# Reordering the first 8 microseconds of a gated attention and MLP kernel: a transpose moved between two groups of products, and the first DMA transpose held longer

## The chip, the cores and the metric

The kernel runs on one core of a Trainium2 chip. The metric is the device time of one execution in microseconds (us). Two forms of it occur below. The *time* is what is compared between kernels. The *span* is what the hardware profiler covers in one profiled execution; the time of that same execution is about 1.7 us longer than its span.

Engines: PE multiplies matrices, PEld is its weight load, DVE and ACT are the vector and scalar engines, POOL is the general engine, SP does nothing here but issue DMAs (SPq in the profile). ACT issues a few DMAs too (ACTq).

## The reference, cut to what matters

```python
x: (1, 2048, 640) bf16
g = sigmoid((x * gate_w).sum(-1))                # gate
qkv = x @ wqkv; q, k, v = ...                    # 32 heads of 20
pk = phi(k)                                      # phi(t) = where(t > 0, t + 1, exp(t)) + 1e-6
kv = einsum("bhsd,bhse->bhde", pk, v)            # linear attention
...                                              # an MLP block b on layernorm(x)
return g * a + (1 - g) * b
```

The kernel starts with K = x @ wk, in 16 chunks of 128 rows of x. A product on PE needs x transposed (the contraction on the partitions), so each chunk has to be transposed, and it needs five slabs of 128 rows of wk.

## The kernel before: the parts that matter

Chunks 0 to 2 are loaded plainly and transposed on PE. Chunks 3 to 15 are transposed by DMA on their way in. All of `late_loads` is issued by SP, one after the other.

```python
for dc in range(3):
    load_wk(aq, dc)                 # K-weight slabs 0, 1, 2, issued by ACT (L162)
load_x(0, 1); load_x(1, 2); load_x(2, 3)        # x chunks 0, 1, 2, issued by SP (L152)
sp.dma_start(wkg[:, 3:5, 0:D], ...)             # slabs 3 and 4 (L169)

def k_mm(c, p, dc):                 # chunk c times slab dc: two matmuls, 512 and 130 columns (L255)
    ...

def late_loads():                   # DMA transposes are load_xT (L155)
    load_xT(3, 4); load_xT(4, 5); load_x(3, 4); load_xT(5, 6); load_xT(6, 7); load_x(4, 6)
    load_xT(7, 8); load_xT(8, 10); load_x(6, 9); load_xT(10, 11); load_xT(11, 13); load_x(9, 12)
    load_xT(13, 16); load_x(12, 16)
    sp.dma_start(wq, ...)           # Q weights (L296), then w1, wv, wo, w2
    ...

def x_tr(c, a, b):                  # chunk c's turn: 5 PE transposes (L321), then two copies
    for dc in range(DC):
        nc.tensor.transpose(t[:, ...], x_sb[:, c, ...], ident[:])
    nc.vector.tensor_copy(xT[:, 0:3, ...], ...)         # L322
    act(xT[:, 3:5, ...], ..., ACT.Copy)                 # L323

x_tr(0, 3, 2)
nc.vector.memset(xT[:, 0, 3 * P:3 * P + 1], 0.0)        # L328
late_loads()
x_tr(1, 1, 2)
k_mm(0, 0, 0); k_mm(1, 1, 0)
k_mm(0, 0, 1); k_mm(1, 1, 1)
x_tr(2, 3, 2)
k_mm(2, 2, 0); k_mm(2, 2, 1)
# ... slabs 2, 3, 4 of chunks 0 to 2; then chunks 3 to 15, with products L264 between; then Q (L388)
```

The memset is a brake. It writes one column of the place that the first DMA transpose (chunk 3) will fill, so that transpose has to wait until the memset is done, and with it everything behind it in SP's queue. The purpose is to keep the DMA transposes, which move in 256-byte packets, off the DMA engines while the first x chunks and slabs load.

## Time and profile before

| | before |
|---|---|
| time, median of 3 | 266.31 us (266.26 to 266.87) |
| time of the profiled execution | 267.08 us |
| span of the profiled execution | 265.4 us |
| PE busy | 259.8 us, 98% |

The busy line of the page of the kernel before (busy us, share of the span, instructions):

```profile
PE 259.8 (98%) x1666; PEld 134.8 (51%) x1666; DVE 127.2 (48%) x227; ACT 109.7 (41%) x163; POOL 35.5 (13%) x118
```

The timeline of PE in the first microseconds of the kernel before. Columns: start, duration, engine, source line, operation, output and inputs, shape, count; in brackets the idle time before it and what ended it.

```profile
4.03 0.62 PE L321 MATMUL pp<-ident,RXH 128*128 128x128 bf16 x5
4.91 0.49 PE L321 MATMUL pp<-ident,RXH 128*128 128x128 bf16 x5 [0.26 <-DMA RXH<-in_A_x_dram]
5.23 0.91 PE L255 MATMUL pp<-RA,RXT 128*128 128x512 bf16 x4
6.69 0.70 PE L255 MATMUL pp<-RA,RXT 128*128 128x512 bf16 x4 [0.55 <-DMA RA<-in_A_wqkv_dram]
7.23 0.44 PE L321 MATMUL pp<-ident,RXH 128*128 128x128 bf16 x5
8.15 0.65 PE L255 MATMUL pp<-RA,RXT 128*128 128x512 bf16 x3 [0.47 <-ACT RXT L323]
```

PE waits 0.55 us for slab 1, multiplies (6.69), transposes chunk 2 (7.23), and waits 0.47 us for the copies of that transpose. After 8.15 us it has no gap worth naming. (The idle time in brackets counts from the modelled end of the instruction before, so a wait costs a little more than it shows: chunk 2's last transpose starts at 7.46 us and the next product at 8.15, 0.69 us later, where transposes otherwise start 0.06 us apart.)

The DMA issues of the kernel before between 1.80 and 2.17 us (KB, then us from issue to landing): x chunk 2, issued at 1.72, and slab 1, issued at 1.79.

```profile
RXH<-in_A_x_dram SPq DMA_DIRECT2D x1, 160.0 KB, 4.7
RA<-in_A_wqkv_dram ACTq DMA_DIRECT2D x1, 160.0 KB, 4.9
```

So chunk 2 landed at 6.44 us and slab 1 at 6.65.

### The profile page before, as it was taken

What the parts mean: (1) busy time and instruction counts of PE and PEld (TensorE: products, weight loads), DVE (VectorE), ACT (ScalarE), POOL (GpSimd) and SP (SyncE); (2) the same over time, 40 slices, a digit from 0 to 9 for tenths busy, and PEclk for the clock granted to TensorE, in tenths of its full rate; (3) what the DMA queues carried; (4) which work ended last, traced back from release to release, by engine and by line L of the source; (5) the groups of instructions that cost most, each with busy time, mean ns of one, the idle gap of its engine ahead of it and who ended that gap; (6) DMA issues with size and microseconds to landing.
All of it is one profiled execution on the core that took longest, in us unless ns stands there. A gap on an engine that the chain in (4) does not pass through costs nothing.

```text
span 265.4 us, 4180 instructions
## 1 busy us (share of the span) xinstructions
PE 259.8 (98%) x1666; PEld 134.8 (51%) x1666; DVE 127.2 (48%) x227; ACT 109.7 (41%) x163; POOL 35.5 (13%) x118
## 2 busy tenths in 40 slices
PE   6999999999999999999999999999999999999995
PEld 2555555555564445554444455555544444555552
DVE  2386659888995257999920044233200002233242
ACT  3466654555454771334977512022034444022020
POOL 7000043030200000446870000000000000000000
PEclk9999999999999999999999999999999999999999
DMA  6899994452252069992542001001000000001001
GB/s 197 162 207 236 367 252 95 99 52 49 50 57 44 11 160 385 340 137 49 108 94 49 0 2 49 25 27 49 27 25 0 0 2 0 25 27 49 25 27 49
DMA packets 42207, 23.95 MB, mean 90 GB/s; under 512 B 31052, under 2 KB 41420, under 8 KB 42188
## 3 DMA queue, kind: packets, MB, share of 16 engines
q1 hardware_dynamic: 41602, 23.16, 36.4%
q10 hardware_dynamic: 586, 0.53, 0.6%
q8 instruction: 13, 0.21, 0.3%
q14 instruction: 6, 0.05, 0.1%
HBM read 12.86 MB, written 3.44 MB: 61 GB/s over the span
## 4 chain that ended last, share of the span: by engine, by line
PE 96%; DMA 2%; DVE 0%; ACTq 0%; ACT 0%; issue 0%
PE pp L637 20%; PE pp L570 20%; PE pp L421 8%; PE pp L596 8%; PE pp L555 8%; PE pp L264 8%; PE pp L255 8%; PE pp L388 8%; DMA RA<-in_A_wqkv_dram 2%; PE pp L579 2%; PE pp L622 1%; PE pp L631 1%; PE pp L586 1%; PE pp L455 1%; PE pp L441 1%; PE pp L468 0%
## 5 line engine op out<-in xcount | busy, mean ns | idle before, releaser
L637 PE MATMUL pp<-RB,RXH 128*128 128x512 bf16 (+1 forms) x390 | 54.4, 299 | 0.0
L570 PE MATMUL pp<-lnxT,RA 128*128 128x512 bf16 x240 | 52.1, 379 | 0.0
L637 PEld LDWEIGHTS <-RXH 128*128 128x128 bf16 x390 | 29.6, 98 | 24.2 <-issue 2.1
L570 PEld LDWEIGHTS <-RA 128*128 128x128 bf16 x240 | 23.4, 98 | 28.1
L599 ACT ACTIVATE RXH<-pp,g_all 128x640 f32<-128x640 f32 x16 | 12.7, 794 | 54.9 <-PE pp L596 54.9
L572 ACT ACTIVATE RXH<-pp 128x1024 bf16<-128x1024 f32 x24 | 24.3, 1020 | 26.7 <-PE pp L570 26.7
L247 ACT ACTIVATE eb<-pp 128x640 bf16<-128x640 f32 (+1 forms) x26 | 21.4, 828 | 25.0 <-PE pp L388 16.1
L264 PE MATMUL pp<-RPK,RXH 128*128 128x512 bf16 (+1 forms) x160 | 25.2, 299 | 0.0
L255 PE MATMUL pp<-RA,RXT 128*128 128x512 bf16 (+1 forms) x160 | 24.1, 299 | 1.0 <-DMA RA<-in_A_wqkv_dram 0.5
L601 DVE SCALAR_TENSOR_TENSOR RPK<-RPK,omg,RXH 128x640 f32<-128x640 f32 x8 | 7.1, 885 | 36.5 <-ACT RXH L599 36.5
L388 PE MATMUL pp<-RXT,RA 128*128 128x512 bf16 x100 | 23.2, 379 | 0.0
L596 PE MATMUL pp<-Mp,pqT 128*128 128x512 bf16 (+1 forms) x160 | 23.1, 299 | 0.0
L555 PE MATMUL pp<-w,RXH 128*128 128x512 bf16 (+1 forms) x160 | 21.9, 299 | 0.0
L601 DVE SCALAR_TENSOR_TENSOR RXT<-RXT,omg,RXH 128x640 f32<-128x640 f32 x8 | 7.1, 885 | 24.6 <-ACT RXH L599 24.6
L421 PE MATMUL pp<-lnxT,RB 128*128 128x512 bf16 x80 | 18.3, 380 | 0.0
L264 PEld LDWEIGHTS <-RXH 128*128 128x128 bf16 x160 | 12.7, 98 | 10.4
L255 PEld LDWEIGHTS <-RXT 128*128 128x128 bf16 x160 | 12.4, 98 | 10.8 <-DVE RXT L322 0.9
L596 PEld LDWEIGHTS <-pqT 128*128 128x128 bf16 x160 | 12.2, 98 | 10.0 <-issue 0.8
L555 PEld LDWEIGHTS <-RXH 128*128 128x128 bf16 x160 | 12.3, 98 | 9.6
L606 DVE SCALAR_TENSOR_TENSOR RXH<-pp,omg,RXT 128x640 bf16<-128x640 f32 x8 | 7.1, 884 | 19.8 <-PE pp L637 19.8
L606 DVE SCALAR_TENSOR_TENSOR RXH<-pp,omg,RPK 128x640 bf16<-128x640 f32 (+2 forms) x9 | 7.3, 810 | 19.1 <-PE pp L637 17.2
L388 PEld LDWEIGHTS <-RA 128*128 128x128 bf16 x100 | 11.1, 117 | 9.1
(107 smaller groups left out, 251.4 us busy)
## 6 DMA issues: line engine op xcount, KB each, us to landing
out_dram<-RXH SPq DMA_DIRECT2D x15, 160.0 KB, 1.8
RA<-in_B_w_dram SPq DMA_DIRECT2D x5, 432.0 KB, 6.7
RA<-in_A_wqkv_dram SPq DMA_DIRECT2D x2, 800.0 KB, 6.8
RB<-in_B_w_dram SPq DMA_DIRECT2D x1, 1120.0 KB
RXH<-in_A_x_dram SPq DMA_DIRECT2D x2, 480.0 KB, 5.1
RB<-in_B_w_dram SPq DMA_DIRECT2D x1, 960.0 KB, 12.2
RB<-in_B_w_dram SPq DMA_DIRECT2D x1, 800.0 KB, 8.5
Mp<-Mscr SPq DMA_DIRECT2D x1, 800.0 KB
```

The costliest lines, as they stand in the source:

```text
L247: act(e[:, 0:n], src, ACT.Exp)
L255: mm(PP[p][:, n0:n1], lhsT=xT[:, dc, c * P:(c + 1) * P], rhs=wkg[:, dc, n0:n1], start=(dc == 0), stop=(dc == DC - 1))
L264: mm(PP[p][:, n0:n1], lhsT=x_sb[:, c, i * P:(i + 1) * P], rhs=pk[:, c, n0:n1], start=(c == 0), stop=(c == NCH - 1))
L388: mm(PP[p][:, tt * 512:(tt + 1) * 512], lhsT=wqp[:, dc, j], rhs=xT[:, dc, t0:t0 + 512], start=(dc == 0), stop=(dc == DC - 1))
L421: mm(PP[p][:, tt * 512:(tt + 1) * 512], lhsT=lh, rhs=lnxT[:, dc, t0:t0 + 512], start=(dc == 0), stop=(dc == DC - 1))
L555: mm(PP[p][:, n0:n1], lhsT=hsT[:, fc, 2 + c * P:2 + (c + 1) * P], rhs=w2[:, fc, n0:n1], start=(fc == 0), stop=(fc == DC - 1))
L570: mm(PP[p][:, k * 512:(k + 1) * 512], lhsT=w3[:, dc, (fc + k) * P:(fc + k + 1) * P], rhs=lnxT[:, dc, t * 512:(t + 1) * 512], start=(dc == ...
L572: act(h2T[:, t % 2, fc:fc + 2, :], PP[p][:].rearrange("p (k s) -> p k s", k=2), ACT.Gelu_apprx_tanh)
L596: mm(PP[p][:, n0:n1], lhsT=pqT[:, j, c * P:(c + 1) * P], rhs=Mp[:, j, n0:n1], start=(j == 0), stop=(j == DC - 1))
L601: nc.vector.scalar_tensor_tensor(x1(c), x1(c), omg[:, c:c + 1], ga, op0=ALU.mult, op1=ALU.add)
L606: nc.vector.scalar_tensor_tensor(oc[:, n0:n1], PP[p][:, n0:n1], omg[:, c:c + 1], x1(c)[:, n0:n1], op0=ALU.mult, op1=ALU.add)
L637: mm(PP[p][:, n0:n1], lhsT=h2T[:, k, fc, cc], rhs=w4[:, fc, n0:n1], start=False, stop=(fc == NF - 1))
```

## The change

The intent: PE does chunk 2's transposes between the slab-0 and the slab-1 products, where it would otherwise wait for slab 1, and the copies run while PE does the slab-1 products. In addition the brake is moved behind chunk 1's turn, so that the DMA transposes start later.

```diff
     x_tr(0, 3, 2)
+    x_tr(1, 1, 2)
     nc.vector.memset(xT[:, 0, 3 * P:3 * P + 1], 0.0)
     late_loads()
-    x_tr(1, 1, 2)
     k_mm(0, 0, 0)
     k_mm(1, 1, 0)
+    x_tr(2, 3, 2)
     k_mm(0, 0, 1)
     k_mm(1, 1, 1)
-    x_tr(2, 3, 2)
     k_mm(2, 2, 0)
     k_mm(2, 2, 1)
```

No instruction is added or removed.

## The prediction

> **What bounds the kernel now.** PE: busy 259.8 us of 265.4 (98%, page), 96% of the chain that ended last. The timeline shows no PE gap over 0.03 us between 8.15 us and the last matmul's end at 262.3 us. All that can be saved lies in the first 8.15 us, where the timeline has three gaps: 0.26 us before chunk 1's transposes (x chunk 1), 0.55 us from 6.15 to 6.69 ("DMA RA<-in_A_wqkv_dram": the second K-weight slab, landing at 6.65), and 0.47 us from 7.68 to 8.15 ("ACT RXT": the copies of chunk 2's turn).
>
> **What the change does.** It adds and removes nothing; the order comparison shows PE's five chunk-2 transposes moved ahead of four K matmuls, and one 59 ns DVE memset moved behind a copy.
>
> 1. Chunk 2's transposes issue 54 to 57 ns apart, 0.28 us for five (the Trainium skill, "TensorE: Matmul & The Clock Gate", Back-to-back issue gap, gives N/2.4 + 2.5 = 56 ns for N = 128; the trace agrees). They now start in the 0.55 us gap, but not at its head: x chunk 2, issued at 1.72 us, lands 4.7 us later by the DMA issue view, at 6.44. PE resumes 0.04 us after a landing, so they run from 6.48 to 6.76.
> 2. Slab-1 products follow: 6.76 to 7.30, against 6.69 to 7.23 before.
> 3. Chunk 2's first product needs both copies. In the trace it starts 0.97 us after the first transpose's weight load (7.18 to 8.15). So 6.48 + 0.97 = 7.45 us instead of 8.15; PE idles 0.15 us instead of 0.47.
> 4. Then 0.54 us of products, and slab 2 is needed at 7.99; it landed at 7.95 before. That just fits. From 6.45 us on 256-byte transpose packets share the DMA engines with the last slab rows; holding them should make slab 2 land earlier.
>
> Gain: 0.70 us, all on the critical path, as PE is gapless afterwards.
>
> **What it costs.** The memset now follows the copy of chunk 1 (5.28 us) instead of chunk 0 (4.57), so the first DMA transpose issues 0.7 us later (4.97 to 5.7). SP issues these back to back (1.2 to 1.3 us per chunk), so the whole load chain slips by 0.7 us while PE comes 0.7 us earlier: each load loses 1.4 us of slack. Landing against first use now: chunk 3 8.55 and 11.1, chunk 5 11.6 and 13.8, chunk 7 15.4 and 17.8, chunks 13 to 15 25.5 and 27.6, Q weights 30.6 and 32.5. The thinnest slack is 1.9 us, so 0.5 us remains. I expect no new wait, but this is the main risk.
>
> **Predicted time:** 266.31 - 0.70 = 265.6 us, 265.1 to 266.3 in 8 of 10. Faster by over 2%: 0.5%; within 2%: 99%; slower by over 2%: 0.5%.
>
> **What would show each step.** Timeline: chunk 2's transposes start near 6.5 us; slab-1 products without a DMA wait; a wait of 0.1 to 0.2 us for the copies; PE gapless from 7.45 us; last matmul near 261.6 us; first DMA transpose issued near 5.7 us; PE idle after 4 us down from 1.3 to about 0.6 us.
>
> **What would make it wrong.** If x chunk 2 lands after 6.65, each tenth costs a tenth of the gain; if by 6.2, the gain could reach 0.9. If slab 2 lands later than 8 us, the wait moves there. If chunk 5, 7, 13 or the Q weights land late, a wait for "RXT<-in_A_x_dram" or "RA<-in_A_wqkv_dram" appears between 10 and 33 us and gives the gain back. The runs before spread 0.6 us, nearly the gain.

## The result

| | before | changed |
|---|---|---|
| time, median of 6 | 266.36 us (266.26 to 266.87) | 265.96 us (265.91 to 266.60) |
| ratio | | 0.9989, interval 0.9976 to 1.0003 |
| span of the profiled execution | 265.4 us | 264.2 us |

A ratio is the mean time of one kernel's fast runs over that of the other's of the same rounds, so it is not quite the ratio of the medians. All runs quoted here were fast, except one of the kernel before in the last group (270.57 us), which the ratios leave out.

The medians differ by 0.40 us, the spans of the two profiles by 1.2. This contradiction is the first thing to explain.

The busy line of the page of the changed kernel, and its PE timeline at the start (32 matmul records are missing from this trace, which is why PE's sum is lower):

```profile
PE 257.8 (98%) x1634; PEld 134.8 (51%) x1666; DVE 127.1 (48%) x227; ACT 109.7 (42%) x163; POOL 35.9 (14%) x118
```

```profile
5.06 0.27 PE L321 MATMUL pp<-ident,RXH 128*128 128x128 bf16 x2 [0.30 <-ACT RXT L323]
5.17 0.71 PE L255 MATMUL pp<-RA,RXT 128*128 128x512 bf16 x4
5.82 0.45 PE L321 MATMUL pp<-ident,RXH 128*128 128x128 bf16 x5
6.11 2.08 PE L255 MATMUL pp<-RA,RXT 128*128 128x512 bf16 x11
```

The chunk-2 transposes now run at 5.82 us, and the products follow without the 0.47 us wait. But they start 0.66 us earlier than the prediction allowed, because chunk 2 landed at 5.77 us instead of 6.44. And chunk 1 had landed at 4.35 us instead of 4.86. Nothing in the change had run by 4.35 us: its first effect is the moved memset, after 4.8 us. So part of the difference between the two profiles is not of the change.

### The profile page after: what moved, and what is told of

Read it like the earlier page. It is cut to its first block, busy times and chain, and to the rows that moved or that the text cites. A ratio compares the mean times of both kernels' runs of the same rounds, so it can differ in the third digit from the quotient of the medians.

```text
span 264.2 us, 4148 instructions
## 1 busy us (share of the span) xinstructions
PE 257.8 (98%) x1634; PEld 134.8 (51%) x1666; DVE 127.1 (48%) x227; ACT 109.7 (42%) x163; POOL 35.9 (14%) x118
## 4 chain that ended last, share of the span: by engine, by line
PE 95%; DMA 2%; issue 1%; ACTq 1%; DVE 0%
PE pp L637 20%; PE pp L570 20%; PE pp L421 8%; PE pp L596 8%; PE pp L264 8%; PE pp L555 8%; PE pp L388 8%; PE pp L255 8%; DMA RA<-in_A_wqkv_dram 2%; PE pp L579 2%; PE pp L622 1%; PE pp L631 1%; PE pp L586 1%; PE pp L455 1%; PE pp L441 1%
## 5 line engine op out<-in xcount | busy, mean ns | idle before, releaser
L637 PE MATMUL pp<-RB,RXH 128*128 128x128 bf16 (+1 forms) x382 | 53.9, 298 | 0.4
L255 PE MATMUL pp<-RA,RXT 128*128 128x130 bf16 (+1 forms) x156 | 23.8, 297 | 0.3
L555 PE MATMUL pp<-w,RXH 128*128 128x128 bf16 (+1 forms) x157 | 21.7, 297 | 0.2
```

What stands on the lines that cost most here:

```text
L255: mm(PP[p][:, n0:n1], lhsT=xT[:, dc, c * P:(c + 1) * P], rhs=wkg[:, dc, n0:n1], start=(dc == 0), stop=(dc == DC - 1))
L555: mm(PP[p][:, n0:n1], lhsT=hsT[:, fc, 2 + c * P:2 + (c + 1) * P], rhs=w2[:, fc, n0:n1], start=(fc == 0), stop=(fc == DC - 1))
L637: mm(PP[p][:, n0:n1], lhsT=h2T[:, k, fc, cc], rhs=w4[:, fc, n0:n1], start=False, stop=(fc == NF - 1))
```

## The experiments

The theory had two parts. **Theory C**: the profile of before caught an execution whose loads landed late. **Theory A**: the moved transposes carry the gain; **rival B**: the longer hold does. A third question came with the second group: what gives gain back later. **Theory D**: the load chain, started later, lands after PE is ready; **rival E**: the landing of the late loads is set by the DMA engines, not by when the chain starts.

Each group of four kernels ran on one chip, with runs of the kernel before among them; the groups ran on different chips. All twelve gave the right result.

For every profile I give the number that decides: the start of chunk 3's first weight load ("chunk 3"), the start of the Q products' first, and their difference. With no wait in between, PE needs 21.38 us for that stretch (eleven of the fourteen profiles show 21.38 or 21.39). What is over 21.38 is called *late wait* below. After the Q products start, every profile needs the same 229.8 to 229.9 us to the last matmul, so nothing later matters.

| profile | first DMA transpose issued | x chunk 2 landed | PE at full clock from | chunk 3 | late wait | Q weights landed | last matmul ends |
|---|---|---|---|---|---|---|---|
| before | 4.97 | 6.44 | 4.43 | 11.09 | 0 | 30.64 | 262.33 |
| changed | 5.20 | 5.77 | 4.29 | 9.93 | 0 | 30.66 | 261.17 |
| b_again | 4.98 | 5.27 | 5.05 | 10.27 | 0 | 30.33 | 261.51 |
| a_again | 5.51 | 5.27 | 5.30 | 9.74 | 0.76 | 31.83 | 261.72 |
| only_move | 4.97 | 5.65 | 4.79 | 9.73 | 0.32 | 31.38 | 261.27 |
| only_hold | 5.38 | 5.30 | 4.67 | 10.27 | 0 | 29.82 | 261.51 |
| m_again | 4.98 | 5.61 | 6.76 | 10.62 | 0 | 30.45 | 261.86 |
| m_nohold | 2.66 | 5.97 | 4.52 | 11.22 | 0 | 29.54 | 262.45 |
| m_early | 4.61 | 5.42 | 4.35 | 9.85 | 0 | 30.04 | 261.09 |
| a_hold2 | 7.42 | 5.74 | 6.87 | 10.51 | 2.08 | 32.07 | 263.82 |
| a_third | 5.51 | 7.42 | 6.44 | 11.33 | 0 | 30.76 | 262.57 |
| a_merge | 5.33 | 7.07 | 4.55 | 10.97 | 0 | 30.90 | 262.22 |
| me_again | 4.61 | 7.11 | 6.25 | 11.02 | 0 | 29.97 | 262.26 |
| me_merge | 4.61 | 5.34 | 5.39 | 9.96 | 0 | 29.79 | 261.20 |

(All in us from the start of the span. Landings are issue time plus the time to landing in the trace. The clock is the moment from which the trace records PE at its full clock.)

Two of these columns vary from execution to execution whatever the kernel: when chunk 2 lands, and when PE's clock goes to full speed. The earliest start of chunk 3 seen is then 10.27 us in the old order (b_again, only_hold) and 9.73 us in the new (only_move, a_again); a late landing or a late clock comes on top. Where chunk 2 landed late, after 6.4 us, the table shows a larger gain: chunk 3 starts 4.65 us after the landing in the old order (before) and 3.90 to 3.91 us after it in the new (a_third, a_merge, me_again), 0.74 us less.

### Group 1: both kernels again, and each half alone

**b_again.** No edit: the kernel before.

> The kernel before, unchanged, for a second profile and for the noise. The two profiles we have differ by 1.16 us in PE's last matmul, the times only by 0.4. Theory C (the first profile of before caught an execution in which the first loads landed late: x chunk 1 at 4.86 us against 4.35 in the changed kernel, before any moved instruction runs): the ratio to before is 1.000 within 0.0015, and a profile of a typical execution has x chunk 1 landing near 4.35, slab 1 near 6.0, and a last matmul near 261.5 us. Rival (the profile is typical and the change itself brought the landings forward): x chunk 1 lands near 4.86 again and the last matmul ends near 262.3.

Measured: 266.57 us against 266.64 for the kernel before in the same group, ratio 1.0003 (0.9990 to 1.0016). Chunk 1 landed at 3.95 us, chunk 2 at 5.27, slab 1 at 5.45, earlier still than expected. PE timeline of b_again:

```profile
5.22 0.27 PE L321 MATMUL pp<-ident,RXH 128*128 128x128 bf16 x2 [0.15 <-ACT RXT L323]
5.33 1.25 PE L255 MATMUL pp<-RA,RXT 128*128 128x512 bf16 x8
6.42 0.44 PE L321 MATMUL pp<-ident,RXH 128*128 128x128 bf16 x5
7.33 0.92 PE L255 MATMUL pp<-RA,RXT 128*128 128x512 bf16 x5 [0.47 <-ACT RXT L323]
```

The 0.55 us wait for slab 1 is gone in the same kernel; the eight products of slabs 0 and 1 run in one piece. Only the 0.47 us wait for the copies remains. Theory C holds: the first profile was of a late-landing execution, 0.82 us worse at the last matmul (262.33 against 261.51). Its time, 267.08 us against a median of 266.31, had said so from the start.

**a_again.** No edit: the changed kernel.

> The changed kernel, unchanged, for a second profile and a tighter time. If the prediction's sum (0.70 us) holds, the ratio to before is near 0.9974. If slab 2's landing now caps the gain, as its 0.09 us wait at 7.44 to 7.54 us in the first profile suggests, the gain is 0.3 to 0.5 us: 0.9981 to 0.9989. The profile should again show a short PE wait for slab 2 (the DMA of the K weights) before the slab-2 products, and none after.

Measured: 266.53 us against 266.64, ratio 0.9999 (0.9981 to 1.0016), with a wide spread (265.72 to 267.49). Both expected ratios were missed. By luck this profile has nearly the same landings up to slab 1 as b_again (chunk 1 at 3.90, chunk 2 at 5.27, slab 1 at 5.46), so the two can be laid side by side. PE timeline of a_again at the start:

```profile
5.21 0.29 PE L321 MATMUL pp<-ident,RXH 128*128 128x128 bf16 x2 [0.15 <-ACT RXT L323]
5.34 0.71 PE L255 MATMUL pp<-RA,RXT 128*128 128x512 bf16 x4
5.89 0.44 PE L321 MATMUL pp<-ident,RXH 128*128 128x128 bf16 x5
6.17 2.10 PE L255 MATMUL pp<-RA,RXT 128*128 128x512 bf16 x13
```

No gap of note after 5.21 us, and chunk 3 starts at 9.74 instead of 10.27: the front gain is 0.53 us. That is the length of the four slab-1 products (0.54 us), which now run while DVE and ACT copy. The short wait for slab 2 that I expected is absent (slab 2 landed at 6.68). But a_again ends 0.21 us *later* than b_again. The weight loads of a_again show why:

```profile
18.23 1.20 PEld L255 LDWEIGHTS <-RXT 128*128 128x128 bf16 x10 [0.29 <-DMA RXT<-in_A_x_dram]
26.81 1.20 PEld L255 LDWEIGHTS <-RXT 128*128 128x128 bf16 x10 [0.57 <-DMA RXT<-in_A_x_dram]
31.88 0.59 PEld L388 LDWEIGHTS <-RA 128*128 128x128 bf16 x4 [0.32 <-DMA RA<-in_A_wqkv_dram]
```

In b_again the same three have no wait:

```profile
18.58 1.24 PEld L255 LDWEIGHTS <-RXT 128*128 128x128 bf16 x10
26.75 1.24 PEld L255 LDWEIGHTS <-RXT 128*128 128x128 bf16 x10
31.65 0.82 PEld L388 LDWEIGHTS <-RA 128*128 128x128 bf16 x5
```

PE is 0.53 us ahead and then waits for the DMA transpose of chunk 8, for that of chunk 13 and for the Q weights. (A weight load's idle time includes a part that is there in any case, since loads run ahead of the products; the late wait proper is 0.76 us, from the table.) The gain was won at the front and given back at 18 to 32 us.

Only part of that lateness is of the longer hold. SP's chain starts 0.53 us after b_again's, but the Q weights landed 1.50 us later (31.83 against 30.33). The rest arises at one place: the DMA transposes of chunk 10 and of chunks 11 and 12, which SP issues one after the other. The SP timeline of b_again, then of a_again:

```profile
14.72 4.04 SPq L155 DMA_TRANSPOSE RXT<-in_A_x_dram  x2
```

```profile
15.22 5.22 SPq L155 DMA_TRANSPOSE RXT<-in_A_x_dram  x2
```

**only_move.** The transposes moved, the brake where it was before.

```diff
     x_tr(0, 3, 2)
-    x_tr(1, 1, 2)
     nc.vector.memset(xT[:, 0, 3 * P:3 * P + 1], 0.0)
     late_loads()
+    x_tr(1, 1, 2)
```

(This diff and the next ones are against the changed kernel, unless said otherwise.)

> Only the five PE transposes of chunk 2 moved; the first DMA transpose is released after chunk 0's copy, as before. Theory A (the moved transposes carry the gain): the ratio equals that of the changed kernel within 0.0005. Rival B (the hold carries it, because 256-byte transpose packets delay the last slab rows): slab 2 lands 0.3 us or more later than in the changed kernel, the wait before the slab-2 products grows by as much, and the gain is 0.1 us or less (0.9996 or more).

Measured: 266.03 us against 266.64, ratio 0.9979 (0.9967 to 0.9991). That is 0.0020 below the changed kernel's ratio, where theory A allowed 0.0005, so neither theory's ratio came true. Chunk 3 starts at 9.73, as early as in a_again, and the late wait is 0.32 us. Theory A holds for the front: the moved transposes alone bring it all. Rival B's mechanism is there in size (slab 2 landed at 7.30 against 6.68 in a_again, of which some may be the execution, as chunk 2 landed later too) but costs nothing to speak of, as PE gets to slab 2 only at about 7.3. SP's timeline of only_move has the same pair of DMA transposes:

```profile
14.68 5.41 SPq L155 DMA_TRANSPOSE RXT<-in_A_x_dram  x2
```

The chain started with b_again's (4.97 us against 4.98) and was level with it up to this pair, which took 1.37 us longer; the Q weights landed 1.05 us later. So the late wait of this profile does not come from a later start. In the other twelve profiles the pair took 3.7 to 4.2 us. Why it took over 5 us in these two is open.

**only_hold.** The brake moved, the transposes where they were; the diff is against the kernel before.

```diff
     x_tr(0, 3, 2)
+    x_tr(1, 1, 2)
     nc.vector.memset(xT[:, 0, 3 * P:3 * P + 1], 0.0)
     late_loads()
-    x_tr(1, 1, 2)
```

> Only the hold: the first DMA transpose waits for chunk 1's copy, PE order as before. Theory A: no gain, ratio 1.000 within 0.0005, since PE still transposes chunk 2 after the slab-1 products and waits about 0.47 us for the copies, and slab 2 has landed by then. Rival B: slab 1 or slab 2 lands earlier by 0.2 us or more and the gain is 0.2 us or more (0.9992 or less).

Measured: 266.66 us against 266.64, ratio 1.0004 (0.9987 to 1.0021). Chunk 3 starts at 10.27, exactly as in b_again, though slab 2 landed 0.34 us earlier (6.69 against 7.03). One pair could be chance, but the table's five profiles in which chunk 2 landed between 5.2 and 5.5 us bear it out: slab 2 landed at 7.41, 7.24, 7.03, 6.69 and 6.68 us where the first DMA transpose was issued at 4.61, 4.61, 4.98, 5.38 and 5.51. The hold does what it is meant to do to the DMA engines and wins nothing here. It agrees with the Trainium skill, "DMA: Bandwidth & Descriptors", Issuing engines are not separate DMA queues: DMAs run on the same 16 engines and interleave, whoever issued them. Slab 2 is issued by ACT, the transposes by SP, and where the transposes were held longer, slab 2 landed earlier.

### Group 2: the start of the load chain, from none to long

**m_again.** No edit to only_move.

> The move without the hold, again, on another chip, as the yardstick of this group. Theory D (the move gains about 0.53 us at the front; the later start of the load chain gives part of it back where chunk 8, chunk 13 and the Q weights land after PE is ready): ratio 0.9975 to 0.9988, PE gapless from about 5.2 us to chunk 13, waits of 0.1 to 0.4 us in all for chunk 13 and the Q weights.

Measured: 266.28 us against 266.76, ratio 0.9987 (0.9968 to 1.0006). In this profile x chunk 1 landed at 5.14 us, the latest of all, and PE reached its full clock only at 6.76. The view of the transposes' line, m_again from 5.0 to 5.75 us and then b_again from 5.1 to 6.5 (count, shortest, median and longest duration in ns), shows the same instruction at the two clocks:

```profile
L321 PE MATMUL pp<-ident,RXH x5: 287/314/314, 5.2 to 5.6; 128*128 128x128 bf16 x5
```

```profile
L321 PE MATMUL pp<-ident,RXH x4: 216/218/219, 5.2 to 6.5; 128*128 128x128 bf16 x4
```

The Trainium skill, "TensorE: Matmul & The Clock Gate", What's actually happening, says that PE starts at half clock and is released after about 3.4 us of activity, at a moment that depends on a free-running window. The trace agrees in kind: 314 ns and then 218, with the step 3.1 to 5.6 us after PE's first matmul at 1.24 us over the fourteen profiles.

So chunk 3 started only at 10.62, and there was no late wait at all. The expected waits did not come, and not only because PE was late. A PE that starts chunk 3 at 9.73 needs chunk 8 at about 18.04 us, chunk 13 at 26.21 and the Q weights at 31.11 (b_again's weight loads, less 0.54); here they landed at 18.00, 25.42 and 30.45. By the same sum only a_again, only_move and a_hold2, of the fourteen profiles, have landings that such a PE would have waited for. An early front makes a late wait longer, but there is none unless the load chain lands late.

**m_nohold.** The move, and no brake at all (diff against only_move).

```diff
     x_tr(0, 3, 2)
-    nc.vector.memset(xT[:, 0, 3 * P:3 * P + 1], 0.0)
     late_loads()
```

> The move, with the artificial memset taken away, so that SP issues the first DMA transpose near 2.7 us. Theory D: the waits for chunk 13 and the Q weights vanish (both land 1.5 to 2.3 us earlier), and what is lost instead is at the front: the 256-byte transpose packets share the DMA engines with x chunk 2 and slabs 1 to 4, which land 0.5 to 1.5 us later, so PE waits there. Net ratio 0.999 to 1.003. Rival E (late waits come from DMA saturation between 15 and 31 us and not from when the chain starts): Q weights land at the same time, 30.3 to 31.8 us, as in the others.

Measured: 266.32 us against 266.76, ratio 1.0001 (0.9972 to 1.0030), spread 265.72 to 268.37. PE timeline of m_nohold:

```profile
6.10 0.44 PE L321 MATMUL pp<-ident,RXH 128*128 128x128 bf16 x5
7.64 1.19 PE L255 MATMUL pp<-RA,RXT 128*128 128x512 bf16 x7 [1.10 <-DMA RA<-in_A_wqkv_dram]
```

Slab 1 landed at 7.60 us and PE waited 1.10 us for it. There is no late wait, as expected, but the front gain is gone too. That speaks for the brake; the times do not separate the two kernels (266.32 us against m_again's 266.28).

Its Q weights landed at 29.54 us, 0.9 before m_again's (30.45) and 1.8 before only_move's (31.38), though the chain started 2.3 us earlier. Neither theory holds strictly: they landed before those of all other profiles, but by less than the earlier start, and by how much differs from profile to profile.

**m_early.** The move, with the brake ahead of chunk 0's copy (diff against only_move).

```diff
+    nc.vector.memset(xT[:, 0, 3 * P:3 * P + 1], 0.0)
     x_tr(0, 3, 2)
-    nc.vector.memset(xT[:, 0, 3 * P:3 * P + 1], 0.0)
     late_loads()
```

> The move, with the memset ahead of chunk 0's copy instead of behind it: the first DMA transpose near 4.6 us, 0.37 earlier. Theory D: late waits shrink to 0.1 us or less, the front keeps its gain as the x and slab loads end near 6.4 to 7.3 us and the transposes' packets start near 6.1 us; ratio equal to the move alone or 0.0005 to 0.001 lower. Rival E: no change of the Q weights' landing.

Measured: 266.03 us against 266.76, ratio 0.9979 (0.9962 to 0.9996). The first DMA transpose is issued at 4.61 us, chunk 3 starts at 9.85, no late wait, and the last matmul ends at 261.09, the earliest of all profiles.

**a_hold2.** The changed kernel with a longer brake: the memset behind chunk 2's turn.

```diff
     x_tr(1, 1, 2)
-    nc.vector.memset(xT[:, 0, 3 * P:3 * P + 1], 0.0)
-    late_loads()
     k_mm(0, 0, 0)
     k_mm(1, 1, 0)
     x_tr(2, 3, 2)
+    nc.vector.memset(xT[:, 0, 3 * P:3 * P + 1], 0.0)
+    late_loads()
```

> The changed kernel with the hold made longer: the first DMA transpose waits for chunk 2's copy (about 6.6 us, 1.1 us later than in the changed kernel's second profile). Theory D: the added hold comes out nearly in full at the end, by longer waits for chunk 8, chunk 13 and the Q weights: last matmul 0.6 to 1.1 us after the changed kernel's, ratio 1.002 to 1.004. Rival E: the Q weights land as before and the ratio stays near 1.000.

Measured: 268.83 us against 266.76, ratio 1.0093 (1.0057 to 1.0129), clear of noise and over twice the loss that theory D expected. PE timeline of a_hold2:

```profile
14.45 1.54 PE L255 MATMUL pp<-RA,RXT 128*128 128x512 bf16 x10 [1.00 <-DMA RXT<-in_A_x_dram]
19.30 1.53 PE L255 MATMUL pp<-RA,RXT 128*128 128x512 bf16 x9 [0.87 <-DMA RXT<-in_A_x_dram]
```

PE waits for chunk 5 (1.00 us) and chunk 7 (0.87). The first DMA transpose came at 7.42 us rather than at the 6.6 I expected, and the waits sit earlier in the chain than expected (chunks 5 and 7, not 8, 13 and Q). Theory D is borne out for the early part of the chain: with its start 1.9 us after a_again's, chunk 5 landed 2.75 us later (14.40 against 11.65), chunk 7 3.25 us later (19.26 against 16.01), and the end of the kernel 2.1 us later. (PE's clock was late here too, full from 6.87 us, so part of that delay was hidden behind a late PE; it did not help, as the loads were later still.) The Q weights, by contrast, landed only 0.24 us later than in a_again. That speaks for rival E, but weakly: a_again's own were late, and against the changed kernel's first profile (30.66) they landed 1.41 us later, for a start 2.22 us later.

### Group 3: is it the issues or the engines?

This group ran on a noisy chip: the kernel before spread from 266.00 to 270.57 us in it, median 267.81. Its ratios separate nothing by themselves; its profiles do.

**a_third.** No edit: the changed kernel.

> The changed kernel a third time, as the yardstick of this group. From its two earlier groups: ratio 0.9985 to 1.0005. Theory D: PE reaches chunk 3 at 9.7 to 10.2 us, and where the first DMA transpose issues at 5.5 us there are late waits of 0.2 to 0.8 us in all.

Measured: 266.26 us against 267.81, ratio 0.9953 (0.9913 to 0.9993), below the expected range. It was expected to reach chunk 3 by 10.2 us; it did at 11.33, because x chunk 2 landed at 7.42 us and slab 1 at 7.63. It has no late wait, though its first DMA transpose issued at 5.51, as in a_again; its Q weights landed at 30.76, 1.07 us before a_again's, so that even an early PE would not have waited for them. Between 5.3 and 7.0 us its DMA engines moved 177 GB/s at a busy share of 0.52, much as a_again's did (161 GB/s, 0.45), where nothing was late. What differs is that from 6.4 us the rows still missing (packets of 1280 bytes) came only about four in each 0.2 us. That looks like one slow engine out of 16, which a landing has to wait for, but the trace does not number the engines, so this is argued, not shown. Landings of chunk 2 after 7 us occur in this group alone (a_third, a_merge, me_again), so the chip may have a part in them.

**a_merge.** The changed kernel with one issue less: two plain x loads merged.

```diff
     load_xT(4, 5)
-    load_x(3, 4)
     load_xT(5, 6)
     load_xT(6, 7)
-    load_x(4, 6)
+    load_x(3, 6)
```

> The changed kernel with the loads of x chunk 3 and of chunks 4 to 5 made one load, at the place of the second: same bytes, one issue of about 0.6 us less on SP. Theory D in its strict form (the late waits are the length of SP's issue chain): the transposes of chunks 7 and later issue 0.6 us earlier than in the changed kernel, the late waits fall by about as much, ratio 0.0015 to 0.0025 below the changed kernel's. Rival E (the DMA engines themselves, not the issues, set the landing of chunk 13 and the Q weights): they land as before within 0.3 us, and the ratio is that of the changed kernel within 0.0008.

Measured: 266.82 us against 267.81, ratio 0.9971 (0.9935 to 1.0007). It is 0.0018 above a_third's, which neither theory expected, but too little to tell on this chip. SP's timeline of a_third, then of a_merge (an entry with x2 is two issues):

```profile
11.99 2.57 SPq L155 DMA_TRANSPOSE RXT<-in_A_x_dram  x2
14.60 0.58 SPq L152 DMA_DIRECT2D RXH<-in_A_x_dram  x1
15.23 3.98 SPq L155 DMA_TRANSPOSE RXT<-in_A_x_dram  x2
```

```profile
11.24 3.28 SPq L155 DMA_TRANSPOSE RXT<-in_A_x_dram  x2
14.56 0.58 SPq L152 DMA_DIRECT2D RXH<-in_A_x_dram  x1
15.19 4.11 SPq L155 DMA_TRANSPOSE RXT<-in_A_x_dram  x2
```

The issue saved puts the chain 0.75 us ahead at chunk 7 (11.24 against 11.99; 0.18 of this is an earlier start). The pair of DMA transposes issued there takes 3.28 us instead of 2.57, and at 15.2 us the two chains are level. The Q weights landed at 30.90 against 30.76. me_merge repeats it: 0.55 us ahead of me_again at chunk 7, behind it at the plain load that follows (14.09 us against 13.70). So rival E holds from about 13 us on, in that shortening the issue chain wins nothing there: SP's issues take the longer. That full DMA engines push them back is argued, not shown. Before that point, as a_hold2 shows, the chain is as late as its start.

**me_again.** No edit to m_early.

> The move with the earlier release again, now beside the changed kernel on the same chip. If the first result holds: ratio 0.997 to 0.9988, below the changed kernel's, no late wait over 0.1 us.

Measured: 266.78 us against 267.81, ratio 0.9958 (0.9916 to 1.0000). It is lower than before but not lower than the changed kernel (0.9953), so this expectation failed; there is no late wait, which held. x chunk 2 landed at 7.11 us here, and PE waited for it:

```profile
7.16 0.45 PE L321 MATMUL pp<-ident,RXH 128*128 128x128 bf16 x5 [0.63 <-DMA RXH<-in_A_x_dram]
```

**me_merge.** m_early with the merged load of a_merge.

> Earlier release and merged load together. If the earlier release has left no late wait, the merge has nothing to win: ratio equal to the earlier release alone within 0.0008. If late waits remain in some executions, up to 0.0015 lower and less spread.

Measured: 266.42 us against 267.81, ratio 0.9957 (0.9918 to 0.9997), equal to me_again within the noise, as expected where no late wait is left.

## Why the prediction was right or wrong

The time, 265.96 us, lies in the predicted range (265.1 to 266.3), and the class (within 2%) was right. The gain was over-stated: 0.70 us predicted, 0.40 measured between the medians of the first chip, about 0.1 on the second (1.55 on the third, which was noisy). That the time fell in the range says little for the mechanism: the range reached to within 0.1 us of no change at all, and the intervals of the ratio on the first two chips include 1.

1. **What bounds the kernel: right.** PE is gapless after the front in every profile except where late loads appear. In the table the last matmul is the start of the Q products plus a constant.
2. **"Chunk 2's transposes ... start in the 0.55 us gap, but not at its head": right for late landings, mis-sized for the others.** The mechanism is right, but the gap is of one execution. In b_again it does not exist (slab 1 landed at 5.45 us, before PE wanted it). In place of the predicted 0.70 us (8.15 to 7.45), the pair with nearly equal landings shows 0.53 us, which is all from hiding the copies behind the slab-1 products. Where chunk 2 landed late, as in the profile that the prediction was made from, the new order saves 0.74 us from its landing to chunk 3 (one profile of the old order against three of the new), which bears the 0.70 out.
3. **"PE idles 0.15 us" for the copies: about right.** 0.09 us in the changed kernel's first profile and in a_again's, by the starts of the products (6.59 to 6.74 us and 6.66 to 6.80, where they are otherwise 0.06 apart).
4. **"Slab 2 ... just fits": right, on the edge.** In the first profile of the changed kernel it landed at 7.49 us and PE idled 0.09 us (7.44 to 7.54). By the starts of the products (7.22 to 7.54, where 0.06 is usual) this wait cost 0.26 us, which is why chunk 3 started at 9.93 there. In a_again it landed at 6.68, before it was wanted. That holding the transposes lands it earlier was right (the five profiles under only_hold), and won nothing in only_hold; what it won in the first profile of the changed kernel, where slab 2 was waited for, is not shown.
5. **"The thinnest slack is 1.9 us, so 0.5 us remains. I expect no new wait": this step failed.** The slacks were read from the late-landing profile, where PE was 0.8 us behind its usual place. In b_again chunk 13 lands at 25.29 us for use at 26.75 and the Q weights at 30.33 for use at 31.65: 1.5 and 1.3 us, not 2.1 and 1.9. Taking 0.53 us (PE earlier) and 0.53 us (first DMA transpose at 5.51 instead of 4.98) from 1.3 leaves 0.2 us, less than the landings vary. a_again shows the result, 0.76 us of late wait in three places, though there the Q weights landed 1.50 us later than in b_again and not 0.53: the transposes of chunks 10 to 12 alone took 1.18 us longer to issue. only_move, without the hold, had 0.32 us for the same reason. This was named as the main risk; what was wrong was the slack, and that it was one execution's.
6. **The hold delays the first DMA transpose by 0.7 us: mis-sized.** By 0.2 to 0.5 us (5.20 and 5.51 against 4.97), since chunk 1 landed before 4.4 us in both profiles and was copied sooner (a little later in a_again, where PE was not at its full clock until 5.30).

So what happened to the gain: 0.53 us is won at the front where chunk 2 lands early, about 0.74 where it lands late; between nothing and 0.76 us is given back between 18 and 32 us, depending on how early PE is and, above all, on how late the chain lands. The move without the hold (0.9979 on the chip where the changed kernel got 0.9999), and with an earlier release (0.9979 on another), keeps more of it in the medians, but the intervals overlap and the noisy chip did not repeat it. That either beats the changed kernel is not shown. What also stays open is why the same DMAs land up to 2 us apart from one execution to the next, why the transposes of chunks 10 to 12 sometimes take over 5 us to issue, and how often an execution has late waits: there is one profile per run, and the timed runs show only their sum.

## What to carry to other kernels

Before costing a change from a profile, compare the profiled execution's own time with the median: here 267.08 against 266.31 meant that one wait in the profile was not typical and that the slacks behind it were 0.5 to 0.6 us too large. A change that brings the busiest engine forward and the loads behind it back spends the same slack twice, so compute what remains from the smallest typical slack and the spread of the landings, not from one profile. Test the two halves of such a change apart: here the reorder carried the front gain, and the longer hold won nothing by itself; that a hold costs time is shown only for the one of a_hold2, which was longer still.

## What the Trainium skill lacked or had wrong

- "DMA: Bandwidth & Descriptors" has no figure for the variation of a landing between executions. Here the same 160 KB load, issued at 1.72 us, landed at 5.27 us in one profile of the changed kernel (a_again) and at 7.42 in another (a_third), and this moved the front of the kernel by 1.6 us. Its section Latency and other measured facts calls DMA engines 7 and 15 usually slower, but ties its best guess at the reason to DMAs that GpSimd issues. Here SP and ACT issue all of them, and no run shows the number of an engine.
- The same page has no issue time of a DMA transpose on trn2 in microseconds. On SP one of 128 x 640 took 1.21 to 1.30 us of the queue in most issues, a plain load of x mostly 0.39 to 0.61 us; a transpose of two chunks took 1.3 us at its quickest and up to 4.2 us.
- No page that I read has this: nearly all DMA traffic stops for over a microsecond. In thirteen of the fourteen profiles 17 or more packets between 17 and 22 us took over 1.0 us each. The stretches of the kernel before, 1.5 us each (duration, then busy time and instructions of each engine, granted clock, DMA share, GB/s), show 17 GB/s at full "busy" share after 207; what causes it is open.

```profile
17.70:19.20 1.50, 1.50 (x14) 0.85 (x12) 1.37 (x3) 1.25 (x4) 0.00 (x0) 1.00 1.29 207
19.20:20.70 1.50, 1.50 (x13) 0.85 (x12) 0.74 (x3) 0.77 (x2) 0.00 (x0) 1.00 1.30 17
```

- "TensorE: Matmul & The Clock Gate", PE-mode transpose, gives about 275 ns for a 128 x 128 transpose in a kernel; at full clock the ones here show 216 to 230 ns and mostly start 55 to 57 ns apart, so five of them cost PE 0.28 us.
- The same page, What you observe, gives the moment of full clock as varying by 0.5 us from run to run; here it varied from 4.29 to 6.87 us over fourteen profiles whose first matmuls are the same.
